# A V scratch read in four row quarters over 128 partitions instead of four shifts over 32

## The chip, the cores and the metric

The kernel runs on one core of a Trainium2 chip. The metric is the device time of one execution in microseconds. A core has TensorE (matmuls), VectorE, ScalarE and GpSimd, each with an instruction queue of its own that runs in order, and SyncE, whose queue here only issues DMAs. ScalarE's queue can issue DMAs too. The transfers themselves run on 16 DMA engines, which serve both issuing queues.

## The reference, cut to what matters

The reference is a transformer block with adaptive layer norms: 2048 tokens of width 512, an attention that looks back over 8 positions 2 apart (32 heads of 16), and a gated feed-forward of width 1792.

```python
mod = (silu(c) @ w_mod).reshape(1, 6, 1, 512)          # sa, ca, ga, sb, cb, gb
h = layernorm(x) * (1 + ca) + sa
x = x + ga * A(h)
h = layernorm(x) * (1 + cb) + sb
x = x + gb * ((gelu(h @ w_gate) * (h @ w_up)) @ w_down)

# A(h): q, k, v = h @ wqkv, 32 heads of 16
# logits[s, w] = q[s] . k[s - 2 w] / 4 for w = 0..7, masked where s - 2 w < 0
# o[s] = sum over w of softmax(logits)[s, w] * v[s - 2 w];  A = o @ wo
```

## The kernel before, in words

**Tiling.** The 2048 tokens are four groups (`sg`) of 512. Inside a group most tiles are transposed: features on partitions, tokens along the row. A group goes through norm 1 (`ln1`), a DMA transpose (`t1`, L466; group 0 on TensorE), scale and shift (`h1`), the matmuls for q, k, v (`qkv`, L520) with their evacuation by ScalarE (`qev`), the logits, the softmax, the weighted sum of V (`pv`), the output matmul (`x1mm`, L717), norm 2 (`ln2`) with its transpose, and the feed-forward (`ffn`, L745 and L758).

**Logits.** The eight shifts w are two halves `wg` of four shifts `w4`. For each half and each quarter `j` of a head, VectorE multiplies q with four shifted windows of k (`pq`, L579). The window pattern steps forward by 2, so entry 0 of `pq` is the largest shift of the half. TensorE sums over features into `LTp` (L594); the four shifts of a half take 32 rows (heads) each, shift `w4` in rows 32 w4 up, for which it takes entry `3 - w4` of `pq`. `LTp` goes through ScalarE (`LT`), a mask (`maskT`, group 0 alone), a DMA transpose (`LN`, L621), the softmax on VectorE and ScalarE, and a transpose back (`PT`, L670).

**V.** The weighted sum needs V in the same form: partition 32 w4 + head, shifted by 2 w4. `vload` (L553 to L566) gets there by way of a scratch in DRAM: the V tile of a group, with a halo of 16 tokens from the group before, is stored to `vscr[sg]` (L555), and four loads (L564) read it back into `V4`, one per shift, each into 32 partitions and the whole row but its first 8 elements: 527.5 KB. Shifts 0 and 1 are issued by SyncE, shifts 2 and 3 by ScalarE; `max_dma_last_dim` cuts each row of 16,880 bytes into four pieces of 4,220. There is one `V4` buffer, so the loads of a group wait until `pv` of the group before has read it. VectorE then multiplies `PT` with `V4` (`pv`, L682) and TensorE sums over the shifts (`o_ps`, L696).

**Order.** Nothing is scheduled by hand. A planner (L54 to L144) runs when the kernel is built. Each step of each stage carries an engine, a price in us, the events that it waits for and the buffer slots that it takes and gives. A stage has a priority per group in the table `PR` (L18; small goes first), and `slack` and `far` say how far ahead of the earliest possible step a more urgent one may be taken on each engine. What comes out is a fixed order of instructions for every queue. Steps that are priced for DMA take a price on the queue and a transfer time `lat`; `hold` keeps SyncE until a transpose has its turn. The order thus depends on all prices and priorities, and on the chip each queue keeps to it, however long a wait lasts.

The other loads on SyncE are x per group (`q_x` and the head), the modulation weights `wm` blocks 0 to 5 (`q_wo`, `q_mb`, `q_gb`), `wo`, `Wg` and `Wu` (`q_gu`), and `WdP`. The modulation matmuls `mb_ps` (L358) and `modT_ps` (L344) wait for the `wm` blocks. `Wg`, `Wu` and `wm` blocks 3 to 5 are only issued once the V loads of group 0 have been issued.

Of the kernel before, what the change touches and what calls it, by code (L numbers as in the profile page):

```python
# [8 lines left out]
ACT = mybir.ActivationFunctionType  # L9
# [6 lines left out]
NEG = -1.0e9  # L16

PR = {  # L18
    "q_wo": 40, "q_x": 11.2, "q_mb": 61.8, "q_gu": 66.2, "q_gb": -14.8, "vh": [34.3, 33, 27, 32.6], "ga":
    102.8, "mb": -3.7, "gb": 9.7, "wds": 3.6, "wos": 33.8, "ln1": [23.2, -12.5, 13.6, 41.2], "t1": [22.4,  # L20
    31.2, 14.5, 36.7], "h1": [-57.1, -20.7, 3.4, 0.4], "qkv": [36.6, -3.8, 37.9, 60.6], "qev": [-15.1, 33,
    29.5, 41.7], "v": [3, 38.2, 2.1, 112], "pq": [3.8, 55, 65.5, 159.8], "lmm": [-8.7, 54.6, 27.9, -1.6],
    "lev": [-14.2, 31.9, 70.3, 21], "smm": [-2.1, -2, 54.7, 29], "soft": [-2.3, 50.2, 112.5, 37.4], "e":
    [32.3, -10.4, 0.4, 61.2], "pt": [33, 40.2, 16.6, 1.3], "pv": [28.8, -8.6, 18, 53.8], "pvmm": [-8.1, 14.1,
    10.4, 5.6], "pvev": [1, 72.5, 71.2, -14.1], "x1mm": [-2.1, 3.7, -1.9, 17.3], "x1": [-8.1, 35.6, -16.2,
    30.1], "ln2": [17.8, 24.5, -2.4, 33.8], "t2": [30.3, 40, 44.4, -0.4], "h2": [13, 2, 38.5, 13.8], "ffn":
    [98.2, 26.9, 31.9, 56], "act": [23.1, 11.8, 16.4, 51], "hh": [-59.6, 31, -10.8, 46.7], "st": [7.9, 31.2,
    1, 2.5],
}


# [22 lines left out]
class Planner:  # L54
# [5 lines left out]
    def __init__(self):  # L60
        self.clock = {e: 0.0 for e in self.LAT}
        self.threads = []
        self.done = {}
        self.slack = {"PE": 0, "ACT": 1.8, "DVE": 1.51, "POOL": 0, "SP": 90.8}
        self.far = {"PE": 0, "ACT": 0, "DVE": 0.49, "POOL": 0, "SP": 33.9}
        self.table = None
        self.quad = False
        self.dma = 0.0
        self.lanes = [0.0] * 8
        self.log = []  # L70
# [77 lines left out]
def kernel(  # L148
# [13 lines left out]
    nc = tc.nc  # L162
    P = 128
    S, D = 2048, 512
    H, DH, W = 32, 16, 8
    F = 1792
    SG = 512
    NSG = S // SG
# [45 lines left out]
    B = {}  # L214

    def setup():
        def f0():
            make_identity(nc, ident[:])
            nc.gpsimd.memset(neghalf[:], -0.5)
        yield Op("POOL", 0.9, f0, fire="ident")  # L220

        def f1():
            nc.gpsimd.memset(M[:], 1.0)
            nc.gpsimd.affine_select(out=M[:], in_=M[:], pattern=[[-4, H]], compare_op=ALU.is_ge, fill=0.0, base=0,
                                    channel_multiplier=1)
            nc.gpsimd.affine_select(out=M[:], in_=M[:], pattern=[[4, H]], compare_op=ALU.is_ge, fill=0.0, base=3,
                                    channel_multiplier=-1)
            nc.gpsimd.memset(maskT[:], 0.0)
            for wg in range(2):
                for w4 in range(4):  # L230
                    w = 4 * wg + w4
                    if w > 0:
                        nc.gpsimd.memset(maskT[32 * w4:32 * w4 + 32, wg, 0:2 * w], NEG)
        yield Op("POOL", 2.0, f1, fire="consts")

        def f2():
            nc.gpsimd.memset(kT[:, :, 0:16], 0.0)
            nc.gpsimd.memset(M2[:], 0.0)
            for w4 in range(4):
                nc.gpsimd.affine_select(out=M2[:], in_=M2[:], pattern=[[-1, H]], compare_op=ALU.not_equal, fill=1.0,  # L240
                                        base=-H * w4, channel_multiplier=1)
        yield Op("POOL", 1.9, f2, fire="M2", after=["LN1.0.rs2"])
# [220 lines left out]
    def transp_dma(key, dkey, dtag, ev):  # L463
        def f():
            B[dkey] = T(dtag, [P, CPS, DT, P], BF16, dtag)
            nc.sync.dma_start_transpose(out=B[dkey][:].rearrange("p c t k -> p (c t) k"),  # L466
                                        in_=B[key][:].rearrange("p c d -> p (c d)"))
        yield Op("SP", 1.8, f, after=[f"{ev}.x3"], take=[SL[dtag]], give=[SL["xn"]], fire=f"{ev}.t", lat=1.9, hold=True)

    def scale_in_place(dkey, sc, bi, ev, dep):  # L470
        for dt in range(4):
# [81 lines left out]
    def vload(sg):  # L553
        def f():
            nc.sync.dma_start(out=vscr[sg][:], in_=B["vT", sg][:])  # L555
        yield Op("SP", 0.65, f, after=[f"vh.{sg}"], give=[SL["vs"]] if sg == NSG - 1 else [], fire=f"vst.{sg}", lat=1.5)
        for n, w4 in enumerate((0, 2, 1, 3)):
            def f(w4=w4):
                if w4 == 0:
                    B["V4", sg] = T("v4", [P, 4 * 4, VL], BF16, "V4")  # L560
                row, skip = 4 * 4 * VL, VH // 2
                d = B["V4", sg][H * w4:H * w4 + H, :, :].rearrange("p r s -> p (r s)")[:, skip:row]
                src = bass.AP(vscr[sg].tensor, vscr[sg].offset + skip - 2 * w4, [[row, H], [1, row - skip]])
                (nc.scalar if w4 > 1 else nc.sync).dma_start(out=d, in_=src, max_dma_last_dim=(row - skip) // 2)  # L564
            yield Op("ACT" if w4 > 1 else "SP", 0.6, f, after=[f"vst.{sg}"], take=[SL["v4"]] if w4 == 0 else [], dma=True,
                     fire=f"V4.{sg}.{n}" if n < 3 else f"V4ld.{sg}", lat=1.45)  # L566

    QB = 2

# [14 lines left out]
    def logits_mm(sg):  # L584
        ps = pairs(sg)
        nb = 2 if sg < QB else 4
        for n in range(0, 8, nb):
            def f(n=n):
                for wg, j in ps[n:n + nb]:
                    if j == 0:  # L590
                        B["LTp", sg, wg] = T("att", [P, SG], F32, "LTp")
                    LTp = B["LTp", sg, wg]
                    for w4 in range(4):
                        nc.tensor.matmul(LTp[32 * w4:32 * w4 + 32, :], lhsT=M[:], rhs=B["pq", sg, wg, j][:, 3 - w4, :],  # L594
                                         start=(j == 0), stop=(j == 3), tile_position=(0, 32 * w4))
            two = ps[n:n + nb]
            wgl, jl = two[-1]
            yield Op("PE", 0.215 * nb, f, quad=True, after=[f"pq.{sg}.{wgl}.{jl}", "consts"], take=[SL["att"]] * sum(j == 0 for _, j in two),
                     give=[SL["prod"]] * nb, fire=f"lp.{sg}.{wgl}" if jl == 3 else None)
        if sg == 0:  # L600
            pl.done["lp.0.0"] = pl.done["lp.0.1"]
# [23 lines left out]
    def soft(sg):  # L625
        def view(g):
            return B["LN", sg][:, g * CPS:(g + 1) * CPS, :].rearrange("p c (w h) -> p c w h", h=H)

        def over_w(t):
            return _ap(t[:, :, 0, :], [[4 * H, CPS], [0, 4], [1, H]])  # L630

        def tree(t, op):
            nc.vector.tensor_tensor(out=t[:], in0=view(0), in1=view(1), op=op)
            nc.vector.tensor_tensor(out=t[:, :, 0:2, :], in0=t[:, :, 0:2, :], in1=t[:, :, 2:4, :], op=op)
            nc.vector.tensor_tensor(out=t[:, :, 0, :], in0=t[:, :, 0, :], in1=t[:, :, 1, :], op=op)

        def f():
            B["mt", sg] = smp["mt"].tile([P, CPS, 4, H], BF16, name="mt")
            tree(B["mt", sg], ALU.max)
        yield Op("DVE", 0.7, f, after=[f"ln.{sg}"] + ([f"p.{sg - 1}"] if sg else []), fire=f"mx.{sg}")  # L640

        def f():
            for g in range(2):
                nc.vector.tensor_tensor(out=view(g), in0=view(g), in1=over_w(B["mt", sg]), op=ALU.subtract)
        yield Op("DVE", 0.66, f, fire=f"z.{sg}")

        def f():
            e = B["LN", sg]
            nc.scalar.activation(out=e[:], in_=e[:], func=ACT.Exp)
        yield Op("ACT", 1.0, f, after=[f"z.{sg}"], act="exp", fire=f"e.{sg}", pr=PR["e"][sg])  # L650

        def f():
            B["sm", sg] = smp["sm"].tile([P, CPS, 4, H], F32, name="sm")
            tree(B["sm", sg], ALU.add)
        yield Op("DVE", 1.15, f, after=[f"e.{sg}"], fire=f"ss.{sg}")

        def f():
            with nc.allow_low_precision(reason="the reference keeps the softmax in this dtype"):
                nc.vector.reciprocal(out=B["mt", sg][:, :, 0, :], in_=B["sm", sg][:, :, 0, :])
        yield Op("DVE", 0.98, f, fire=f"ri.{sg}")  # L660

        def f():
            for g in range(2):
                nc.vector.tensor_tensor(out=view(g), in0=view(g), in1=over_w(B["mt", sg]), op=ALU.mult)
        yield Op("DVE", 0.66, f, fire=f"p.{sg}")

    def soft_out(sg):
        def f():
# [187 lines left out]
```

## Time and profile before

| | |
|---|---|
| three runs | 254.89 us median (253.73 to 256.72) |
| profiled execution | 254.05 us, its span 252.2 us |
| busy: TensorE, VectorE, ScalarE, GpSimd | 232.4, 178.4, 140.0, 14.2 us |
| DMA | 31.74 MB, mean 126 GB/s |
| V loads | 16 of 527.5 KB, median 9.2 us (ScalarE's) and 9.7 us (SyncE's) from issue to landing |
| scratch stores | 4 of 528.0 KB, median 4.2 us to landing |
| first FFN matmul | 82.39 us |

Times in a profile count from the start of the span. A row of slices has 40 digits, each the busy share of 6.3 us in tenths; PEclk is the clock that TensorE was granted, in tenths of full speed. The chain lists what the end of the program can be followed back to; a row is start, length and what ran or was waited for. A row of DMA queues gives packets, megabytes and the share of 16 engines' time in the stretch asked for; q1 is the queue that SyncE issues on, q10 that of ScalarE.

### The profile page before, as it was taken

The page shows a single profiled execution, that of the slowest core. Times are in us where ns is not written, and L with a number is a line of the kernel's source. Part 1 is how long each engine was busy: PE and PEld are TensorE (multiplying, and loading weights), DVE is VectorE, ACT ScalarE, POOL GpSimd, SP SyncE. Part 2 cuts the span into 40 slices and gives each one's busy share as a digit, 9 for nine tenths or more (in the row PEclk, how much of TensorE's full clock was granted, in tenths as well). Part 3 has the DMA queues.
Part 4 walks back from the last instruction along what each step waited for, and adds up shares of the span by engine and source line. Part 5 has one row for each costly group of instructions (what it writes and reads, how often), then busy time and mean ns, then how long its engine had stood idle before and what let it go on. Part 6 is the DMA issues. An engine that isn't in the chain of part 4 may idle for free.

```text
span 252.2 us, 3509 instructions
## 1 busy us (share of the span) xinstructions
PE 232.4 (92%) x1278; PEld 102.8 (41%) x1292; DVE 178.4 (71%) x313; ACT 140.0 (55%) x233; POOL 14.2 (6%) x37
## 2 busy tenths in 40 slices
PE   7897980498999999999999999999999999999994
PEld 2452440134444433444444444444444444444441
DVE  4789929798989999989999978547949622222222
ACT  2365835539467987634564836925772640766400
POOL 4310103000030000001000001000000100000000
PEclk9999998589999999999999999999999999999999
DMA  6939699999999095760520852503000041000011
GB/s 206 353 109 263 189 231 190 245 192 409 330 313 213 0 263 114 165 182 21 125 62 4 221 122 44 105 21 83 3 1 0 9 98 52 12 0 0 3 42 42
DMA packets 38153, 31.74 MB, mean 126 GB/s; under 512 B 23928, under 2 KB 34424, under 8 KB 38136
## 3 DMA queue, kind: packets, MB, share of 16 engines
q1 hardware_dynamic: 36976, 27.20, 41.6%
q10 hardware_dynamic: 1160, 4.32, 6.7%
q8 instruction: 10, 0.16, 0.3%
q14 instruction: 7, 0.06, 0.1%
HBM read 21.49 MB, written 4.26 MB: 102 GB/s over the span
## 4 chain that ended last, share of the span: by engine, by line
PE 76%; DMA 9%; SPq 5%; DVE 4%; ACT 3%; issue 2%; ACTq 0%
PE y_ps L758 19%; PE u_ps L745 19%; PE g_ps L745 19%; PE qkv_ps L520 8%; PE x_ps L717 5%; DMA x<-in_A_x_dram 3%; DMA wm<-in_w_mod_dram 3%; PE o_ps L696 3%; SPq L466 3%; PE LTp L594 2%; DVE pq L579 2%; DMA h<-xn 2%; SPq L263 1%; PE mb_ps L358 1%; ACT h L474 1%
## 5 line engine op out<-in xcount | busy, mean ns | idle before, releaser
L745 PE MATMUL g_ps<-h,Wg 128*128 128x512 bf16 x224 | 57.5, 379 | 0.5 <-ACT gl L769 0.5
L745 PE MATMUL u_ps<-h,Wu 128*128 128x512 bf16 x224 | 57.6, 379 | 0.0
L769 ACT ACTIVATE gl<-g_ps 128x512 bf16<-128x512 f32 x56 | 33.6, 600 | 32.5 <-PE g_ps L745 28.2
L758 PE MATMUL y_ps<-WdP,hht 128*128 128x512 bf16 x217 | 48.6, 379 | 0.4
L520 PE MATMUL qkv_ps<-hT,wqkv 128*128 128x512 bf16 x191 | 45.1, 386 | 0.4 <-ACT hT L492 0.3
L787 DVE TENSOR_TENSOR hht<-gl,ub 128x512 bf16<-128x512 bf16 x56 | 23.3, 422 | 28.2 <-ACT ub L776 27.7
L776 ACT CAST ub<-u_ps 128x512 bf16<-128x512 f32 x56 | 32.9, 587 | 16.1 <-PE u_ps L745 16.0
L682 DVE TENSOR_TENSOR pv<-PT,V 128x2048 bf16<-128x2048 bf16 x32 | 37.6, 1219 | 2.6 <-PE mb_ps L358 1.4
L579 DVE TENSOR_TENSOR pq<-qT,kT 128x2048 bf16<-128x2048 bf16 x32 | 37.8, 1218 | 1.0 <-PE o_ps L696 1.0
L745 PEld LDWEIGHTS <-Wg 128*128 128x128 bf16 x224 | 21.6, 98 | 27.9 <-issue 2.5
L758 PEld LDWEIGHTS <-hht 128*128 128x128 bf16 x224 | 22.0, 98 | 26.4
L745 PEld LDWEIGHTS <-Wu 128*128 128x128 bf16 x224 | 21.3, 98 | 27.8 <-issue 3.0
L520 PEld LDWEIGHTS <-wqkv 128*128 128x128 bf16 x192 | 21.0, 115 | 23.2 <-issue 5.6
L794 DVE TENSOR_TENSOR ot<-y_ps,x 128x512 bf16<-128x512 f32 x16 | 11.0, 690 | 24.1 <-PE y_ps L758 24.1
L424 DVE BATCH_NORM_STATS2 st<-x 128x6 f32<-128x512 bf16 x32 | 21.6, 675 | 3.7 <-DMA x<-in_A_x_dram 3.6
L434 POOL TENSOR_TENSOR rstd<-rstd,neghalf 128x4 f32<-128x4 f32 (+1 forms) x9 | 10.3, 1150 | 182.3 <-DVE rstd L430 182.3
L474 ACT ACTIVATE h<-h,modT,scl 128x512 bf16<-128x512 bf16 x16 | 11.7, 801 | 7.1 <-DMA h<-xn 7.1
L717 PE MATMUL x_ps<-woP,oT 128*128 128x512 bf16 x60 | 14.1, 379 | 0.2
L535 ACT CAST qT<-qkv_ps 128x512 bf16<-128x512 f32 x16 | 9.5, 591 | 7.3 <-PE qkv_ps L520 7.1
L474 ACT ACTIVATE hT<-hT,modT,scl 128x512 bf16<-128x512 bf16 x12 | 8.8, 803 | 8.1 <-DMA hT<-xn 8.1
L358 PE MATMUL mb_ps<-wm,scT 128*128 128x512 bf16 x7 | 2.9, 521 | 10.5 <-DMA wm<-in_w_mod_dram 10.5
L726 DVE TENSOR_TENSOR x<-x_ps,x 128x512 bf16<-128x512 f32 x16 | 10.9, 683 | 2.0 <-PE x_ps L717 1.9
(62 smaller groups left out, 143.9 us busy)
## 6 DMA issues: line engine op xcount, KB each, us to landing
V<-vscr ACTq DMA_DIRECT2D x8, 527.5 KB, 9.2
V<-vscr SPq DMA_DIRECT2D x8, 527.5 KB, 9.7
wm<-in_w_mod_dram SPq DMA_DIRECT2D x6, 512.0 KB, 5.8
vscr<-vT SPq DMA_DIRECT2D x4, 528.0 KB, 4.2
out_dram<-ot SPq DMA_DIRECT2D x16, 128.0 KB, 1.7
Wg<-in_B_w_gate_dram SPq DMA_DIRECT2D x1, 1792.0 KB, 8.7
Wu<-in_B_w_up_dram SPq DMA_DIRECT2D x1, 1792.0 KB, 13.7
WdP<-in_B_w_down_dram SPq DMA_DIRECT2D x1, 1792.0 KB, 8.4
```

The costliest lines, as they stand in the source:

```text
L424: nc.vector.bn_stats(out=st_k["st"][:, c4, :], in_=src()[:, c4, :])
L474: nc.scalar.activation(out=h, in_=h, func=ACT.Identity, scale=sc(dt), bias=bi(dt))
L520: nc.tensor.matmul(ps[:].rearrange("p (c k) -> p c k", k=P), lhsT=wqkv[:, blk, dt, j:D:4], rhs=hview(B["hT", sg], dt), start=(dt == 0), st ...
L579: nc.vector.tensor_tensor(out=pq[:], in0=_ap(B["qT", sg][:, j, :], [[0, 4], [1, SG]]), in1=_ap(kT[:, j, k0:k0 + SG], [[2, 4], [1, SG]]), o ...
L682: nc.vector.tensor_tensor(out=t[:], in0=_ap(B["PT", sg][:, CPS * wg, :], [[0, 4], [1, SG]]), in1=B["V4", sg][:, j:16:4, c0:c0 + SG], op=AL ...
L717: nc.tensor.matmul(ps[:], lhsT=B["oT", sg][:, j, c4 * P:(c4 + 1) * P], rhs=woP[:, j, :], start=(j == 0), stop=(j == 3))
L745: nc.tensor.matmul(ps[:].rearrange("p (c k) -> p c k", k=P), lhsT=Wt[:, dt, ft * P:(ft + 1) * P], rhs=hview(B["h2T", sg], dt), start=(dt = ...
L758: nc.tensor.matmul(ps[:], lhsT=B["hh", sg, ft][:, c4 * P:(c4 + 1) * P], rhs=B["WdP"][:, ft, :], start=(ft == 0), stop=(ft == FT - 1))
L769: nc.scalar.activation(out=gl[:], in_=B["g", sg, ft][:], func=ACT.Gelu_apprx_tanh)
L776: nc.scalar.copy(out=ub[:], in_=B["u", sg, ft][:])
L787: nc.vector.tensor_tensor(out=hh[:], in0=B["gl", sg, ft][:], in1=B["ub", sg, ft][:], op=ALU.mult)
L794: nc.vector.tensor_tensor(out=ot[:], in0=B["y", sg, c4][:], in1=B["x", sg][:, c4, :], op=ALU.add)
```

## The change

The four reads of a group's scratch are cut the other way. Each now covers all 128 partitions (four shifts of 32 rows) and a quarter of the row: 2,110 elements, 4,220 bytes per partition. All four are issued by SyncE. The source pattern walks the shifts with a step of +2 elements, so the partitions hold the shifts in reverse order; the logits' sums and the mask are put in that order as well. The bytes and the number of contiguous pieces per load stay as they were. Besides, prices in the planner, its slack and all priorities are other numbers.

```diff
 PR = {
-    "q_wo": 40, "q_x": 11.2, "q_mb": 61.8, "q_gu": 66.2, "q_gb": -14.8, ...
-    "t1": [22.4, 31.2, 14.5, 36.7], ... "v": [3, 38.2, 2.1, 112], ... "t2": [30.3, 40, 44.4, -0.4], ...
+    "q_wo": 70, "q_x": 8, "q_mb": 29.9, "q_gu": 69.4, "q_gb": 1.8, ...
+    "t1": [-5.7, 8, -4.9, -4.5], ... "v": [25.2, 26.8, -2, 10.2], ... "t2": [33.9, -5.3, 23.4, 21.3], ...
...
-        self.slack = {"PE": 0, "ACT": 1.8, "DVE": 1.51, "POOL": 0, "SP": 90.8}
-        self.far = {"PE": 0, "ACT": 0, "DVE": 0.49, "POOL": 0, "SP": 33.9}
+        self.slack = {"PE": 0.25, "ACT": 0.43, "DVE": 14.23, "POOL": 0, "SP": 109.36}
+        self.far = {"PE": 0, "ACT": 0, "DVE": 0.26, "POOL": 0, "SP": 36.16}
...
-                        nc.gpsimd.memset(maskT[32 * w4:32 * w4 + 32, wg, 0:2 * w], NEG)
+                        nc.gpsimd.memset(maskT[32 * (3 - w4):32 * (3 - w4) + 32, wg, 0:2 * w], NEG)
...
-        yield Op("SP", 0.65, f, after=[f"vh.{sg}"], ..., fire=f"vst.{sg}", lat=1.5)
-        for n, w4 in enumerate((0, 2, 1, 3)):
-            def f(w4=w4):
-                if w4 == 0:
+        yield Op("SP", 0.65, f, after=[f"vh.{sg}"], ..., fire=f"vst.{sg}", lat=1.0)
+        for n in range(4):
+            def f(n=n):
+                if n == 0:
                     B["V4", sg] = T("v4", [P, 4 * 4, VL], BF16, "V4")
                 row, skip = 4 * 4 * VL, VH // 2
-                d = B["V4", sg][H * w4:H * w4 + H, :, :].rearrange("p r s -> p (r s)")[:, skip:row]
-                src = bass.AP(vscr[sg].tensor, vscr[sg].offset + skip - 2 * w4, [[row, H], [1, row - skip]])
-                (nc.scalar if w4 > 1 else nc.sync).dma_start(out=d, in_=src, max_dma_last_dim=(row - skip) // 2)
-            yield Op("ACT" if w4 > 1 else "SP", 0.6, f, after=[f"vst.{sg}"], ..., lat=1.45)
+                step = (row - skip) // 4
+                a = skip + n * step
+                src = bass.AP(vscr[sg].tensor, vscr[sg].offset + a - 6, [[2, 4], [row, H], [1, step]])
+                nc.sync.dma_start(out=B["V4", sg][:].rearrange("p r s -> p (r s)")[:, a:a + step], in_=src)
+            yield Op("SP", 0.55, f, after=[f"vst.{sg}"] + ([f"V4ld.{sg - 1}"] if sg else []), ..., lat=1.35)
...
-                        nc.tensor.matmul(LTp[32 * w4:32 * w4 + 32, :], lhsT=M[:], rhs=B["pq", sg, wg, j][:, 3 - w4, :],
+                        nc.tensor.matmul(LTp[32 * w4:32 * w4 + 32, :], lhsT=M[:], rhs=B["pq", sg, wg, j][:, w4, :],
...
```

The planner's prices of the DMA transposes (`lat` 1.9 to 2.1) and of four softmax steps (0.7 to 0.92, 0.66 to 0.68, 1.15 to 1.38, 0.98 to 0.88) are changed in the same way; they alter no instruction, only the order that the planner finds.

## The prediction

> **What bounds the kernel now.** I read the 40 slices first, then the chain that ended last, then SyncE's own order of time around the hole that they show. The slices of the page (tenths of 6.3 us each):
>
> ```profile
> PE   7897980498999999999999999999999999999994
> PEclk9999998589999999999999999999999999999999
> DMA  6939699999999095760520852503000041000011
> ```
>
> TensorE has one hole, slices 6 to 7 (about 37 to 50 us), with its granted clock at half in it. From about 57 us on it is full to the end; the chain names TensorE for nearly all that follows 86.5 us. The DMA engines are full from 25 us to 82 us. So a change in the DMA work of the first 86 us moves the end almost one for one, while later DMA work lies under matmuls. The chain, in order of time, inside the hole (start us, us, what):
>
> ```profile
> 36.37 0.61 PE mb_ps L358 x2
> 36.98 5.88 SPq L466
> 42.96 4.42 DMA wm<-in_w_mod_dram
> 47.42 1.90 PE mb_ps L358 x4
> ```
>
> TensorE stands 10.45 us on the load of wm block 5. SyncE's order of time says why that load came late:
>
> ```profile
> 30.61 1.01 SPq L564 DMA_DIRECT2D V<-vscr  x2
> 32.31 10.55 SPq L466 DMA_TRANSPOSE hT<-xn  x1
> 42.96 0.53 SPq L276 DMA_DIRECT2D wm<-in_w_mod_dram  x1
> ```
>
> The transpose of group 2 holds SyncE for 10.55 us, against 1.92 us for the same instruction at 118.74 us, where no V load is in flight: it stands behind the four V loads of group 0 (two from SyncE, two from ScalarE at 30.16), and the wm load behind it. The V loads are thus on the path, and their duration is the main term.
>
> **The new read.** First the old one alone. Group 2's four loads at 101.7 us run with no other data load; the DMA rows of the stretch 100 to 115 us (packets, MB, share of 16 engines):
>
> ```profile
> q10 hardware_dynamic: 288, 1.08, 28.8%
> q1 hardware_dynamic: 288, 1.08, 28.2%
> ```
>
> 57.0% of 15 us is 8.55 us of all 16 engines for 2.16 MB: 253 GB/s, 15.8 GB/s per engine. That is slow. The rows of two stretches (PE, PEld, DVE, ACT, POOL, clock, DMA share, GB/s):
>
> ```profile
> 58.00:64.00 6.00, 5.81 (x52) 2.89 (x54) 4.97 (x5) 5.92 (x15) 0.00 (x0) 1.00 1.03 407
> 101.70:112.00 10.30, 10.25 (x53) 4.37 (x53) 9.10 (x19) 4.61 (x9) 0.00 (x0) 1.00 0.84 212
> ```
>
> At 58 to 64 us the weights Wg and Wu, into 128 partitions, move at 407 GB/s, 25.4 GB/s per engine. If the new read ran like them, a group would take 2.16 MB / 407 = 5.3 us, 3.25 us less than now. The Trainium skill, "SBUF — State Buffer", section "The DMA port swizzle", says that a transfer into partitions 0 to 31 reaches only 8 of 16 ports and measured 189 GB/s at 1 MiB; the 253 GB/s of two queues at once fits that in kind, and its rule alone would give the faster read.
>
> But how many engines does the new read use? The packets tell. 288 for two loads is 144 per load: 32 partitions in four pieces of 4,220 bytes are 128, and 16 are left, which I read as one closing packet for each engine used. The load of c, which is issued on the same queue in the first 4 us, is the only one whose outermost dimension is 4:
>
> ```profile
> q10 hardware_dynamic: 8, 0.00, 0.1%
> ```
>
> Eight packets: four rows, and four closing ones, not 16. In these two rows the closing packets follow the outermost dimension, 4 for 4 and 16 for 32. The new source pattern is [[2, 4], [row, 32], [1, step]]: its outermost dimension is 4 (the shifts), though the destination's is 128. I take four engines of 16. Against it: c has four rows on both sides, so its row cannot show what a 4 against 128 does. The Trainium skill, "DMA: Bandwidth & Descriptors", section "Why a DMA increments its semaphore by 16 and not by 1", says that the engine count is the largest number up to 16 that divides the slowest dimension of both sides, and the lowest-numbered engines are taken; that makes 4 here, and the same four for every V load. By that rule the sum is the one below; c's row agrees with it, and no row here has sides that differ.
>
> A load stays 540,160 bytes in 128 pieces. On four engines at 25.4 GB/s it takes 540,160 / 101.6 GB/s = 5.3 us, a group 21.3 us; at 15.8 GB/s, if the slowness lies in the source, 8.55 and 34.2 us. A single engine's pieces now lie in one quarter of the partitions, without 15 others in the same 32, so I take the weight loads' rate and keep the other for the top. Against 8.55 us: **+12.7 us per group**, +25.6 at the top, -3.25 if all 16 run, 0 if all 16 run at the old rate.
>
> **What of that reaches the end.** Group 0: its loads can start no sooner than now, 30.2 us (the scratch store issued at 26.5 lands 3.0 later). They land near 30.2 + 21.3 + 2 = 53.5. The planner orders SyncE by priority among steps it already knows. It prices the four loads at 4 x 1.35, and the transpose of group 2 depends on a VectorE norm that ends at 32.2 in the trace, so I expect V before that transpose again, though its priority (-4.9) is now ahead of V's (25.2). Then the transpose, the wm block 5, PT of group 0 and all behind wait 12.7 us more, since each spreads over all engines and ends with its share on the four. TensorE has done qkv of group 1 by 36 us and has nothing else but qkv of group 2, which needs that transpose; wherever the new priorities put mb, the hole grows by 12.7. This I take: +12.7. If the transpose goes ahead, only pv of group 0 is late (starting at 49.5 now, 53.5 at best): +4.
>
> Group 1: loads wait for the single V buffer, free when pv of group 0 ends (58.7 now), then the last lands near 77, and pv of group 1 starts at 90.75: 13.8 us of cover, just over 12.7. What is not covered is SyncE's transpose of h for group 0 (issued 74.40, landing 4.3 later, then the ACT h that FFN waits for): behind V of group 1 it costs from 0 to another 12.7. I take 0, by the 13.8 us of cover and because that buffer wait moves with everything else, and keep 12.7 for the range.
>
> Groups 2 and 3: V issues at 101.7 and 138.8 to 145.5, pv starts at 129.26 and 172.28: 27.5 and 26.8 us between the last issue and the use, more than 21.3 + 2. LN of group 3 (151.40) stands behind V of group 3 and may move by 12.7, and pv with it, but FFN of group 3 starts at 212.56 and its x_ps is done at 191.85. Covered: 0. If it weren't, one more 12.7.
>
> **The small edits.** Eight issues at 0.36 us leave ScalarE's queue (2.9 us in all, most of it where ScalarE waits on TensorE: 0) and eight at 0.42 join SyncE's, whose queue waits tens of us on VectorE: 0, and 1.7 us in the two head groups if SyncE were full. The reversed shifts change the index of pq, the mask's partitions and V's rows alike, with the same instructions: 0. The scratch store and the planner's prices change no instruction's own length. The new priorities reorder all engines; no row prices that. Bounds: the hole of 10.45 us (with 2 us of half clock after it) is the most that a better order can win, and the same size is what a worse one can lose; I take 0, since after 86.5 us TensorE has no hole to win from.
>
> **Sum.** On the profiled execution's own time, 254.05 us (span 252.2 and 1.85 around it; the median of the runs is 254.89): 254.05 + 12.7 = 266.8 us, +5.0%. Its own range: 258 (only pv late) to 280 (group 1 uncovered too, or the slow rate: 254.05 + 25.6).
>
> **The rivals.**
> - *All 16 engines, full rate.* Each group's loads take 5.3 us. The transpose and wm come 3.25 us sooner in the hole, and V of group 1 gives 0 to 3.25 more to the path: 254.05 - 3.25 to -6.5, 249.2 in the middle. For it: the destination has 128 partitions, and 253 GB/s now beside 407 for a transfer of that form. Against it: c's four closing packets. It decides as soon as a V load shows 16 closing packets. Chance 0.22. This is the other side.
> - *All 16 engines, the old rate* (the slowness lies in the short-shifted DRAM source): the change does not do what it says, and only the new order is left: 254 give or take 3. For it: nothing shows where the 15.8 GB/s comes from. Chance 0.06.
> - *Four engines, but the new order hides them*: hT of groups 2 and 3 ahead of V (their priorities are now -4.9 and -4.5), TensorE running qkv of both during V, and the 10.45 us hole filled: 254.05 + 4 - up to 10.45 = 248 to 258. For it: those priorities; against it: VectorE must do two norms before pv, and pv still has no V before 53.5. Chance 0.10.
> - Forecast: four engines, on the path: 0.62.
>
> **Numbers.** A measurement of this kernel tells about 1% from nothing (253.73 to 256.72). Faster by over 1%: 0.19 of the first rival, 0.01 of the second, 0.05 of the third: 0.25. Within 1%: 0.02, 0.03, 0.03: 0.08. Slower: 0.62 and the rest, 0.67. The range leaves out the first rival's lower half and the forecast's top: 248.5 to 281.
>
> **What would show it.** A V load of 132 packets (128 and 4) instead of 144, landing over 15 us after issue where it runs alone as the last of four (9.5 now), a DMA share near a quarter and about 100 GB/s in group 2's V stretch; the hole in TensorE before qkv of group 2 or before o_ps of group 0 longer than 10.45 us; FFN's first matmul near 95 us instead of 82.4; an unbroken TensorE after it. 144 packets and over 350 GB/s in that stretch would make the prediction wrong at its first step; four engines with FFN starting by 84 us at its last.

## The result

The changed kernel takes **299.81 us** (median of four runs, 298.98 to 302.35), against 255.16 us for the kernel before in the same comparison: a ratio of 1.177, interval 1.167 to 1.186. It is slower by 45 us where 12.7 were forecast. The profiled execution has a span of 300.5 us, against 252.2.

The slices of the page after, each now 7.5 us, as before in tenths:

```profile
PE   8894970039999109999992999999499999999995
PEclk9997796559999755999998699999779999999999
DMA  7939392299683969501294200293320004100001
```

TensorE has two holes ahead of the feed-forward instead of one (around 43 to 65 us and 98 to 112 us), and two notches after it that before has not. The clock falls at each of them. The DMA row, which stood at 9 tenths through most of the first third before, now falls to 2 to 3 tenths there, and in later places where V loads run. The chain shows what the holes wait for (start us, us, what):

```profile
42.85 17.32 SPq L465
60.27 4.51 DMA wm<-in_w_mod_dram
...
90.04 21.53 DMA h<-xn
...
151.68 12.37 DMA h<-xn
...
206.11 6.21 DMA h<-xn
```

The hole ahead of qkv of group 2 is the one of before, made longer. The others are new: three transposes of `h`, for groups 0, 1 and 2, that took 4.3 us from issue to landing before. The chain of before has the one of group 0:

```profile
74.40 4.27 DMA h<-xn
```

SyncE's own order of time after shows what stands ahead of each:

```profile
35.20 4.50 SPq L564 DMA_DIRECT2D V<-vscr  x4
39.82 20.35 SPq L465 DMA_TRANSPOSE hT<-xn  x1
...
77.56 5.25 SPq L564 DMA_DIRECT2D V<-vscr  x3
82.85 0.59 SPq L262 DMA_DIRECT2D Wu<-in_B_w_up_dram  x1
90.04 19.56 SPq L465 DMA_TRANSPOSE h<-xn  x1
...
136.94 4.47 SPq L564 DMA_DIRECT2D V<-vscr  x4
151.68 10.32 SPq L465 DMA_TRANSPOSE h<-xn  x1
...
184.57 5.63 SPq L564 DMA_DIRECT2D V<-vscr  x4
...
206.11 4.16 SPq L465 DMA_TRANSPOSE h<-xn  x1
```

Every one of these transposes comes next, or nearly next, behind a group's V loads, and holds the queue until those have drained: in group 2 the DMA share stays at a quarter until 162 us, and the hold ends there. TensorE's waits, in total (us, times, longest):

```profile
PE mb_ps L357 <- DMA wm<-in_w_mod_dram: 24.2, 2, 22.0
...
PE g_ps L745 <- ACT h L473: 23.3, 4, 14.1
```

The second line is 0 before. The first matmul of the feed-forward starts at 112.54 us, 30.2 later than before; from there to the end it is 188.0 us, against 169.8. Of those last 18 us, 9.2 are waits (5.33, 1.14 and 2.70) and about 8.1 are slower matmuls: the groups `g_ps` and `u_ps` are busy 62.9 and 60.3 us, against 57.5 and 57.6, for the same 448 matmuls.

**How many engines.** The page's rows of packets after, and the row of the stretch 139 to 151 us, where the four V loads of group 2 run with little else (PE, PEld, DVE, ACT, POOL, clock, DMA share, GB/s):

```profile
q1 hardware_dynamic: 37936, 31.52, 51.8%
...
q10 hardware_dynamic: 8, 0.00, 0.0%
```

```profile
139.00:151.00 12.00, 12.00 (x57) 5.49 (x56) 11.25 (x28) 5.42 (x8) 1.38 (x1) 1.00 0.26 88
```

The two queues had 36,976 and 1,160 packets before. Together that is 192 more than now, and 192 is 16 loads of 12 packets: a V load closes with 4 packets instead of 16. A quarter of the engines' time is busy although four loads are in flight, so the four loads use the same four engines. That stretch moves 59 to 89 GB/s in each us up to 146 us and 101 to 110 from there on.

### The profile page after: what moved, and what is told of

Same layout as the page of the kernel before. It is cut to its first block, busy times and chain, and to the rows that moved or that the text cites. A ratio compares the mean times of both kernels' runs of the same rounds, so it can differ in the third digit from the quotient of the medians.

```text
span 300.5 us, 3514 instructions
## 1 busy us (share of the span) xinstructions
PE 244.1 (81%) x1292; PEld 104.3 (35%) x1292; DVE 178.6 (59%) x313; ACT 142.2 (47%) x233; POOL 16.6 (6%) x37
## 2 busy tenths in 40 slices
DMA packets 37961, 31.74 MB, mean 106 GB/s; under 512 B 23736, under 2 KB 34232, under 8 KB 37944
## 4 chain that ended last, share of the span: by engine, by line
PE 65%; DMA 20%; SPq 9%; ACT 3%; DVE 1%; issue 1%; ACTq 0%
PE u_ps L745 17%; PE g_ps L745 17%; DMA h<-xn 13%; PE y_ps L758 11%; PE qkv_ps L519 9%; SPq L465 6%; PE x_ps L717 5%; DMA wm<-in_w_mod_dram 4%; DMA x<-in_A_x_dram 3%; PE o_ps L696 3%; ACT h L473 3%; PE LTp L594 2%; SPq L262 1%; PE mb_ps L357 1%; SPq L268 1%
## 5 line engine op out<-in xcount | busy, mean ns | idle before, releaser
L745 PE MATMUL g_ps<-h,Wg 128*128 128x512 bf16 x224 | 62.9, 398 | 24.2 <-ACT h L473 23.3
L745 PE MATMUL u_ps<-h,Wu 128*128 128x512 bf16 x224 | 60.3, 393 | 0.0
L682 DVE TENSOR_TENSOR pv<-PT,V 128x2048 bf16<-128x2048 bf16 x32 | 38.1, 1220 | 21.9 <-DMA PT<-LN 17.9
L787 DVE TENSOR_TENSOR hht<-gl,ub 128x512 bf16<-128x512 bf16 x56 | 23.6, 422 | 28.4 <-ACT ub L776 27.9
L745 PEld LDWEIGHTS <-Wu 128*128 128x128 bf16 x224 | 22.0, 100 | 31.1 <-issue 7.8
L433 POOL TENSOR_TENSOR rstd<-rstd,neghalf 128x4 f32<-128x4 f32 (+1 forms) x9 | 12.5, 1385 | 229.7 <-DVE rstd L429 229.7
L357 PE MATMUL mb_ps<-wm,scT 128*128 128x512 bf16 x8 | 3.8, 628 | 24.2 <-DMA wm<-in_w_mod_dram 24.2
L473 ACT ACTIVATE hT<-hT,modT,scl 128x512 bf16<-128x512 bf16 x12 | 8.9, 803 | 20.4 <-DMA hT<-xn 20.4
L633 DVE TENSOR_TENSOR mt<-LN 128x512 bf16<-128x512 bf16 x4 | 1.7, 424 | 23.1 <-DMA LN<-LT 23.1
L440 DVE TENSOR_SCALAR xn<-x,mv,rstd 128x512 bf16<-128x512 bf16 x32 | 11.3, 407 | 1.8 <-POOL rstd L433 1.7
```

The costliest lines, as they stand in the source:

```text
L473: nc.scalar.activation(out=h, in_=h, func=ACT.Identity, scale=sc(dt), bias=bi(dt))
L682: nc.vector.tensor_tensor(out=t[:], in0=_ap(B["PT", sg][:, CPS * wg, :], [[0, 4], [1, SG]]), in1=B["V4", sg][:, j:16:4, c0:c0 + SG], op=AL ...
L745: nc.tensor.matmul(ps[:].rearrange("p (c k) -> p c k", k=P), lhsT=Wt[:, dt, ft * P:(ft + 1) * P], rhs=hview(B["h2T", sg], dt), start=(dt = ...
L787: nc.vector.tensor_tensor(out=hh[:], in0=B["gl", sg, ft][:], in1=B["ub", sg, ft][:], op=ALU.mult)
```

## The experiments

**Three patterns under one plan.** The first two runs keep every order of after and change only the source's dimensions. Bytes, pieces and destination partitions stay.

```diff
-src = bass.AP(vscr[sg].tensor, vscr[sg].offset + a - 6, [[2, 4], [row, H], [1, step]])
+src = bass.AP(vscr[sg].tensor, vscr[sg].offset + a - 6, [[row, H], [2, 4], [1, step]])          # 32 outermost
+src = bass.AP(vscr[sg].tensor, vscr[sg].offset + a - 6, [[4 * row, 8], [2, 16], [1, step]])     # 8 outermost
```

> After, with its plan untouched; only the source pattern of the four V loads is turned, [[row, 32], [2, 4], [1, step]] for [[2, 4], [row, 32], [1, step]]: the outermost dimension is 32, the same 540,160 bytes in the same 128 pieces go to the same 128 partitions, but head-major, so V meets the weights of other heads and shifts (this part of the computation is changed; the work is the same). Theory E (the engine count follows the source's outermost dimension, and that is the whole loss): 144 packets per load again, about 5.3 us of all engines per group (2.16 MB at 407 GB/s), the holds of 20.4, 19.6 and 10.3 us on the transposes gone, 246 to 256 us. Theory O (the new order of work is to blame, or four queues' worth of issues on SyncE): still above 280 us.

> As the turned pattern, but with an outermost dimension of 8: [[4 row, 8], [2, 16], [1, step]] (V's rows are those of eight heads at sixteen shifts, so this part of the computation is changed; bytes and pieces are the same). Theory E: 136 packets per load, eight engines, 2.16 MB at 203 GB/s = 10.6 us per group, 2 us more than the old read's 8.55: 250 to 264 us, between the two others. Theory O: no nearer to before than after is.

Measured: 253.62 us with 32 outermost (ratio 0.996, 0.993 to 1.000), 269.78 us with 8 (1.063, 1.056 to 1.070), 299.81 us with 4. The packets of the whole program are 38,136, 38,008 and 37,944 on the two queues: 144, 136 and 132 per V load. The V loads and the transposes behind them, on SyncE, with 32 outermost:

```profile
35.70 2.53 SPq L564 DMA_DIRECT2D V<-vscr  x4
38.34 6.47 SPq L465 DMA_TRANSPOSE hT<-xn  x1
...
75.22 2.01 SPq L465 DMA_TRANSPOSE h<-xn  x1
```

and with 8:

```profile
34.42 2.96 SPq L564 DMA_DIRECT2D V<-vscr  x4
37.49 12.84 SPq L465 DMA_TRANSPOSE hT<-xn  x1
...
81.19 10.88 SPq L465 DMA_TRANSPOSE h<-xn  x1
```

The hold of the same transpose is 6.47, 12.84 and 20.35 us for 16, 8 and 4 engines, and the time follows. The source's outermost dimension is the cause of the loss, and it is all of it: with 32 there, after is no slower than before. The run with 8 missed its range (250 to 264). I had reckoned with 25.4 GB/s per engine; its stretch of group 2's V (121 to 131 us) has

```profile
121.00:131.00 10.00, 9.95 (x47) 4.50 (x46) 9.35 (x22) 4.53 (x8) 1.20 (x1) 1.00 0.51 143
```

half the engines' time and 143 GB/s, which is 17.9 per engine. The four engines of after start slowly too: their 88 GB/s over the 12 us shown above are 22 each, and only from 146 us on do they move 25 to 27 each (101 to 110 GB/s). Why eight are slower apiece over most of the load (sixteen shifts of the same row, or two engines in each 32 partitions) was not tried.

**The read alone, and the plan alone.** Before with only the new read, and after with the old read:

```diff
 # read_only: before, plus the reversed mask and logits
-src = bass.AP(..., vscr[sg].offset + skip - 2 * w4, [[row, H], [1, row - skip]])
+src = bass.AP(..., vscr[sg].offset + a - 6, [[2, 4], [row, H], [1, step]])
 # plan_only: after
-src = bass.AP(..., vscr[sg].offset + a - 6, [[2, 4], [row, H], [1, step]])
-nc.sync.dma_start(out=..., in_=src)
+src = bass.AP(..., vscr[sg].offset + skip - 2 * (3 - i), [[row, H], [1, row - skip]])      # i = 0, 2, 1, 3
+nc.sync.dma_start(out=d, in_=src, max_dma_last_dim=(row - skip) // 2)
```

> Before, with its plan and its two issuing queues, and only the new read (four row quarters, outermost dimension 4, shifts in reverse order in V, the logits and the mask). Theory E: 21.3 us per group on four engines; +12.7 us at the hole before qkv of group 2, and the transposes of h for groups 0 to 2 late behind V by 6 to 10 us each where 5 us or less of cover is left: 270 to 295 us. Theory O: the read alone costs 12.7 us or less, 254 to 268 us.

> After, with its plan and all issues on SyncE, but each load again one shift into 32 partitions, the whole row in four pieces (in the order of partitions that after has). Theory E: 144 packets per load, 8.5 us per group, 252 to 260 us: the plan alone is worth less than 2%. Theory O: 280 us or more. If one queue alone makes the old read slower (two shifts in flight at once would have used more of the chip), a group takes up to 11 us and the time is 258 to 265.

Measured: 301.89 us for the read alone (1.188, 1.181 to 1.195) and 258.82 us for the plan alone (1.019, 1.014 to 1.025). The read alone costs what the whole change costs, 7 us beyond its range; in it, too, transposes stand behind V, though they are not all the same ones. From SyncE's order of time of the read alone:

```profile
33.59 22.53 SPq L466 DMA_TRANSPOSE hT<-xn  x1
...
86.52 18.79 SPq L466 DMA_TRANSPOSE h<-xn  x1
...
148.54 8.18 SPq L466 DMA_TRANSPOSE h<-xn  x1
...
188.09 7.63 SPq L623 DMA_TRANSPOSE LN<-LT  x1
```

The plan alone is within its range but 5.2 us above the same plan with 32 outermost. Both use 16 engines, in pieces of the same size; a load fills 32 partitions in the plan alone and 128 with 32 outermost. TensorE's hole before qkv of group 2 is 11.34 us in the first and 6.71 in the second, a difference of 4.6 us. The rows of group 2's V stretch, 15 us each (packets, MB, share of 16 engines), first the plan alone, then 32 outermost:

```profile
q1 hardware_dynamic: 576, 2.16, 66.7%
```

```profile
q1 hardware_dynamic: 576, 2.16, 40.9%
```

That is 10.0 us of all engines for a group's V, 216 GB/s, against 6.1 us, 352 GB/s, with the same packets. So the read into 128 partitions is faster, as the change has it, as long as it uses 16 engines; and the old read takes longer on one queue than on two (8.55 us before). The Trainium skill, "SBUF — State Buffer", section "The DMA port swizzle", has 189 and 328 GB/s for 32 and 128 partitions in transfers of 1 MiB; the ratio here is 1.63, there 1.74.

**Which group costs what.** The plan of after with four engines in some groups and 32 outermost in the others:

```diff
-    [[2, 4], [row, H], [1, step]])
+    [[2, 4], [row, H], [1, step]] if sg == 0 else [[row, H], [2, 4], [1, step]])      # first_group
+    [[2, 4], [row, H], [1, step]] if sg > 1 else [[row, H], [2, 4], [1, step]])       # late_groups
```

> The plan of after; four engines (outermost dimension 4) in group 0 alone, the turned pattern (outermost 32, 16 engines, V's rows head-major, so that V meets other weights there) in groups 1 to 3. The prediction's step for group 0 (12.7 us at the hole before qkv of group 2): against the turned pattern everywhere (253.6 us) the hold of group 2's transpose goes from 6.5 back to 20.4 us, 13.9 more, and all of it reaches the end: 265 to 269 us. If the whole loss of 46 us came from group 0 by a chain that it starts: 285 or more.

> The plan of after; four engines in groups 2 and 3 alone, the turned pattern (V's rows head-major there) in groups 0 and 1. The prediction's step (covered, 0): 252 to 256 us. The rival from the trace of after (the transposes of h for groups 1 and 2 stand behind V of groups 2 and 3 and FFN waits for them): 9 to 14 us more than the turned pattern everywhere, 262 to 268 us.

Measured: 268.67 us with four engines in group 0 (1.056, 1.054 to 1.058), 15.0 us above the 253.62 with none. SyncE, around group 0's V and at the `h` transpose of group 0:

```profile
38.68 19.63 SPq L465 DMA_TRANSPOSE hT<-xn  x1
...
89.20 1.82 SPq L465 DMA_TRANSPOSE h<-xn  x1
```

One long hold, and the chain behind it without a further loss. The run for groups 2 and 3 gave 265.32, 269.90, 270.91 and 271.68 us, too far apart for an interval, but 12 to 18 us above none, not the 0 of the prediction. Its profiled execution (269.9 us):

```profile
37.75 6.47 SPq L465 DMA_TRANSPOSE hT<-xn  x1
...
118.19 10.80 SPq L465 DMA_TRANSPOSE h<-xn  x1
...
167.10 6.16 SPq L621 DMA_TRANSPOSE LN<-LT  x1
173.37 4.16 SPq L465 DMA_TRANSPOSE h<-xn  x1
```

The four times of this run lie 6 us apart, so the lowest, 12 us above none, is what it shows at the least. Of the 46.2 us between 4 and 32 outermost, 15.0 belong to group 0 and 12 to 18 to groups 2 and 3; if the parts add up, 13 to 19 are left for group 1, which was not run by itself. Its part can still be read from the traces. Ahead of the first feed-forward matmul, the run with group 0 alone and after differ in group 1's loads only. That matmul, with 32 outermost everywhere, with four engines in group 0, and in after:

```profile
83.48 1.03 PE L745 MATMUL g_ps<-h,Wg 128*128 128x512 bf16 x4
```

```profile
97.47 1.03 PE L745 MATMUL g_ps<-h,Wg 128*128 128x512 bf16 x4
```

```profile
112.54 2.70 PE L745 MATMUL g_ps<-h,Wg 128*128 128x512 bf16 x4 [14.08 <-ACT h L473]
```

So group 0 costs 14.0 us up to there and group 1 another 15.1, most of it the hole of 14.08 us. From that matmul to the end of the span the first two take 169.1 us and after 188.0; these 18.8 us belong to groups 2 and 3 and to the matmuls at half the clock right behind group 1's hole.

**V behind the transposes of h.** After, four engines, with the loads of groups 1 to 3 put behind the `h` transpose on SyncE, and no other order changed:

```diff
     def transp_dma(key, dkey, dtag, ev):
         def f():
             nc.sync.dma_start_transpose(...)
+            if dtag == "h2":
+                turned.add(key[1])
+                for g in held.pop(key[1] + 1, []):
+                    g()
...
+            def f(read=read):
+                if sg == 0 or sg - 1 in turned:
+                    read()
+                else:
+                    held.setdefault(sg, []).append(read)
```

> After, four engines in all groups; only V's loads of groups 1 to 3 are taken out of their place in SyncE's order and put right behind the transpose of h of the group before; every other queue keeps its order. If V ahead of h is what costs in groups 1 to 3: the holds of 19.6, 10.3 and 4.2 us on those transposes fall to about 2, and 20 to 32 us are won: 267 to 280 us. If the four engines hold up whatever comes next (LN and PT stand behind V then, and V comes too late for pv): 285 to 300 us.

Measured: **332.05 us** (1.302, 1.293 to 1.311), 32 us slower than after, above even the second range. Taking V from its place ahead of `h` wins nothing. The holds on `h` did go, and the next in line took them over. SyncE's order of time, and two of the waits on VectorE:

```profile
90.47 2.06 SPq L465 DMA_TRANSPOSE h<-xn  x1
92.58 5.77 SPq L570 DMA_DIRECT2D V<-vscr  x4
98.44 15.58 SPq L632 DMA_TRANSPOSE LN<-LT  x1
```

```profile
DVE ot L805 <- DMA out_dram<-ot: 40.9, 2, 22.8
...
DVE mt L644 <- DMA LN<-LT: 21.7, 2, 21.4
```

Group 1's V now holds up the logits' transpose, for which VectorE waits 21.4 us. V of groups 2 and 3 now stands ahead of the output stores; VectorE's next output tile needs a stored one's buffer and waits 22.8 and 18.1 us for it, with the feed-forward's own multiplications queued behind. Whatever comes behind 21 us of V on those four engines is late, and much of what comes behind is needed at once.

**V on the other queue.** After, with all V loads issued by ScalarE:

```diff
-                nc.sync.dma_start(out=B["V4", sg][:]..., in_=src)
+                nc.scalar.dma_start(out=B["V4", sg][:]..., in_=src)
```

> After, four engines in all groups, SyncE's and all other orders kept, but the V loads are issued by ScalarE's queue, so that they no longer stand ahead of the transposes on the queue that issues these. If a transpose waits because its queue is in order: its hold falls to 2 to 5 us, and the time to 262 to 280. If each of the four engines takes packets of the two queues in turn, a transpose, whose packets are many and short (under 512 bytes), still waits for about one 4,220 byte packet per own packet: holds of 12 to 20 us, 285 to 300 us.

Measured: 310.22 us (1.219, 1.215 to 1.224), above both ranges. SyncE's transposes, no longer behind V on their own queue:

```profile
35.97 14.81 SPq L465 DMA_TRANSPOSE hT<-xn  x1
...
93.50 20.47 SPq L465 DMA_TRANSPOSE h<-xn  x1
```

The holds stay at 14.8 and 20.5 us, which speaks against the order of one queue as the reason. It fits a wait for the four engines themselves; that packets of the two queues take turns on them is argued, not shown. The fourth issue of group 1 also kept ScalarE's queue for 6.39 us, with the scale of `hT` behind it.

**A version to keep, with 16 engines.** The plan of before, 32 outermost in the source, so that V's partitions are 4 head + shift. The softmax's last multiplication brings the weights into that order:

```diff
-nc.vector.tensor_tensor(out=view(g), in0=view(g), in1=over_w(B["mt", sg]), op=ALU.mult)
+hm = B["PN", sg][:, g * CPS:(g + 1) * CPS, :].rearrange("p c (h w) -> p c w h", w=4)
+nc.vector.tensor_tensor(out=hm, in0=view(g), in1=over_w(B["mt", sg]), op=ALU.mult)     # head_major
...
+hm = B["PN", sg][:, g * CPS:(g + 1) * CPS, :].rearrange("p c (h w) -> p c h w", w=4)
+per = _ap(B["mt", sg][:, :, 0, :], [[4 * H, CPS], [1, H], [0, 4]])
+nc.vector.tensor_tensor(out=hm, in0=view(g).rearrange("p c w h -> p c h w"), in1=per, op=ALU.mult)   # head_major_read
...
-nc.tensor.matmul(o_ps[H * i:H * i + H, :], lhsT=M2[:], rhs=B["pv", sg, j, wg][:, i, :],
+nc.tensor.matmul(o_ps[H * i:H * i + H, :], lhsT=M[:], rhs=B["pv", sg, j, wg][:, i, :],
```

> A version to keep: the plan and the two issuing queues of before, with the turned pattern (128 partitions, outermost dimension 32, 16 engines), and the rest made to fit it: the softmax's last multiplication writes its weights head-major into a second tile, which the transpose back reads, and the sum over shifts takes the 4-to-1 matrix Mph in place of Msum. Theory E: about 6 us of all engines per group instead of 8.55, the hole before qkv of group 2 shorter by 2.5 to 4.3 us: 249 to 252 us. Rival: the strided write on VectorE (420 ns for 512 elements now) takes twice as long and gives it back, 0.8 us per group in the softmax chain: 252 to 255 us.

> The head-major version once more (plan of before, turned pattern on 16 engines), with the order change moved from the write to the read of the softmax's last multiplication: it now writes the second tile element after element and reads the weights 32 apart. In the version with the strided write each of the eight multiplications took 1,324 ns instead of 420. If the strided write is what gave the gain back: 420 to 700 ns each, 1.2 to 1.8 us less per group in the softmax chain, 250 to 252.5 us. If a strided read costs as much as a strided write: about 1,300 ns each and 253 to 254.5 us, as in the version before.

Measured: 253.67 us (0.9955, 0.9925 to 0.9986) and 253.91 us (0.9971, 0.9945 to 0.9997). Both beat before, by 0.45 and 0.3 per cent, and both lie in the range of the poorer of their two cases, the second with a cheaper multiplication than that case had. The multiplication, in the two versions (busy us, mean ns of one; 420 before):

```profile
L668 DVE TENSOR_TENSOR pn<-LN,mt 128x512 bf16<-128x512 bf16 x8 | 9.8, 1324 | 0.1
```

```profile
L669 DVE TENSOR_TENSOR pn<-LN,mt 128x512 bf16<-128x512 bf16 x8 | 7.7, 1008 | 0.1
```

A strided write takes 3.2 times as long as the plain one, a strided read 2.4 times. That is 1.2 to 1.8 us per group, but it isn't all: the second version is no faster than the first. In the second, the V loads of group 2 take 6.0 us of all engines, the hole ahead of qkv of group 2 is 7.44 us instead of 10.45, and at 83.59 us the kernel is 2.9 us ahead of before (86.53) on the same feed-forward matmul. Then, on TensorE:

```profile
91.36 0.40 PE L701 MATMUL o_ps<-pv,Mph 128*32 128x512 bf16 x4 [0.49 <-DVE pv L687]
92.83 0.40 PE L701 MATMUL o_ps<-pv,Mph 128*32 128x512 bf16 x4 [1.07 <-DVE pv L687]
...
105.07 2.54 PE L722 MATMUL x_ps<-woP,oT 128*128 128x512 bf16 x11
```

TensorE now waits for VectorE's `pv` of group 1, which before was ready in time, and at the output matmuls it leads by 0.9 us (105.07 against 105.97). So 2.0 of the 2.9 us are lost on the way, 1.6 of them in these two waits. VectorE has little room there: it is busy 27.9 of the 30 us from 80 to 110, and was busy 28.9 of them before.

## Why the prediction was wrong, point by point

**The hole before qkv of group 2, and the four engines: right.** That later DMA work lies under matmuls was not (see groups 2 and 3). c's four closing packets did mean that the engine count follows the outermost dimension, and here the smaller side decides. A V load has 132 packets and the stretch a quarter of the engines, both as forecast; it moves 88 GB/s over its 12 us, and the forecast 100 only in its second half. The Trainium skill, "DMA: Bandwidth & Descriptors", section "Why a DMA increments its semaphore by 16 and not by 1", states the rule that the prediction cites; these runs agree with it for 4 against 128, 8 against 128 and 32 against 128. The rival of 16 engines with its 249 us is refuted for this kernel. With the source turned it came out at 253.62 us, not at 249: its hole is 6.71 us instead of the 10.45 of before, yet its first feed-forward matmul comes at 83.48 us, 1.1 later than before. What in the new order takes the gain back was not traced.

**Group 0, +12.7 us: nearly right.** The hold on group 2's transpose grew from 10.55 to 20.35 us and TensorE's wait from 10.45 to 22.0; four engines in group 0 alone cost 15.0 us against 16 engines, where my 12.7 + 3.25 would have been 15.95.

**Group 1, "I take 0": this is the step that failed first.** The 13.8 us of cover were `pv`'s. The transpose of `h` has none: it is next but one behind V on SyncE, and TensorE runs out of qkv at 98.5 us. It landed 21.5 us after issue instead of 4.3, a new hole of 14.08 us opened, and the first feed-forward matmul came 15.1 us later than with four engines in group 0 alone. I had named that transpose and priced it up to 12.7, and then chosen 0 on the ground of a wait that is not its own.

**Groups 2 and 3, "Covered: 0": wrong by 12 to 18 us.** I checked V against its own reader (27 us of room, which was enough) and `LN` of group 3, and never asked which transposes come behind V on SyncE. Those of `h` for groups 1 and 2 do, 10.32 and 4.16 us of hold, and the feed-forward of the next group begins with them. "After 86.5 us TensorE has no hole to win from" is true, but it has no slack to lose either.

**What the sum left out.** Each hole costs more than its length, since the clock falls in it. In after the granted clock is 0.50 from 102 to 118 us, the first four feed-forward matmuls in there take 2.70 us instead of 1.03, and in all 8.1 of the 48 us between the two profiles are slower feed-forward matmuls. The prediction had seen 2 us of half clock behind the hole of before, but put nothing for it into the sum.

**The small edits and the plan: right in size.** The same plan with 16 engines is at 0.996 of before, and the plan with the old read is 1.9% slower than before. How much of that is the single queue (10.0 us of all engines for a group's V instead of 8.55) was not separated from the order.

## What to carry to other kernels

A DMA's speed depends on which dimension of each side is outermost, not only on how many partitions it fills: count the closing packets of a load, or look at whether the DMA share stands at a quarter, before a pattern with 4 on the outside goes into a loop. When a transfer gets longer, list everything that is issued behind it and ask for each what TensorE does until it lands; the transfer's own reader may be the one with the most room. And a shorter transfer only pays as far as the next engine is idle: here two thirds of the gain in the hole were lost again within 22 us, most of it in waits for VectorE.

## What the runs showed of the hardware that was not expected

- A transpose issued on SyncE's queue waits about as long behind loads that ScalarE's queue issued (holds of 14.8 and 20.5 us) as behind its own (20.4 and 19.6), when the loads run on four engines.
- Eight engines moved 17.9 GB/s each over 10 us of a group's V; four moved 22 each over 12 us, 25 to 27 in the later part.
- A bf16 `TENSOR_TENSOR` of 128x512 took 420 ns contiguous, 1,008 ns with one input read 32 elements apart and each element of the other read four times in a row, 1,324 ns with the output written 4 elements apart.
- With four loads outstanding on one queue and on four engines, the fourth issue itself took long: SyncE's longest V issue was 4.07 us. With 16 engines under the same plan it was 1.51 us, and before, with two loads on each queue, every one took 0.31 to 0.53.
